# Backward part of a decode step on one NeuronCore: V blocks that TensorE transposes, taken as 32-bit words

## The chip, the cores and the metric

The program runs on one NeuronCore of a Trainium2 chip. A core has TensorE (PE, matrix products; its weight loads are listed as PEld), VectorE (DVE), ScalarE (ACT), GpSimd (POOL) and SyncE (SP), which here issues nearly all of the transfers between the device memory (HBM) and the on-chip memory (SBUF). PE writes its products to a small accumulator memory (PSUM). The metric is the device time of one execution, in microseconds.

## The reference

One decode step of a transformer block: layer norm, attention of one query per head over a cache of 4096 keys and values, a gated feed-forward part, and all gradients of it. Four sequences, 32 heads, head size 128, all in bf16:

```python
scores = jnp.einsum("bhqd,bhkd->bhqk", q, k_cache) * (Dh ** -0.5)
p = _softmax(scores, axis=-1)
o = jnp.einsum("bhqk,bhkd->bhqd", p, v_cache)
return ... @ wo
...
h = x + _A_ref(_layernorm(x), k_cache, v_cache, wq, wo)
h2 = h + _B_ref(_layernorm(h), w1, w3, w2)
```

What is returned is `h2` and the gradients for the input, both caches and all weights. The gradient of the V cache is, for each of the 128 pairs of sequence and head, the outer product of P (4096 numbers) and dO (128 numbers). The gradient of the K cache is the outer product of dS and q, with dS = P * (dP - c) * scale, where dP is the product of the head's V (4096 x 128) with dO, and c is one number for a head. A head's K, V and each of its two cache gradients hold 1 MB. So 128 MB of K are read once, 128 MB of V twice (once in the forward part, once for dP), and 256 MB of gradients are written.

## The kernel before

SBUF holds an arena of 23 slots of about 1 MB (`Slot`); a pair of neighbouring slots (`Slot2`) takes 2 MB. The order of the work on each engine is the order of the program text; every engine and SP's transfer queue go through their own list in that order and wait where data or space is missing. Which slot a tile gets is settled when the program is made, by the age of the free slots.

The forward part, up to about 655 us, streams K and V. A middle part (to about 703 us) computes the feed-forward part and the gradient dO for the first eight heads of each sequence. The backward part follows, and the change lies in it.

Heads 0 to 31 (`SP = 32`) are handled one at a time, the other 96 as 48 pairs. For a head, `load_V2` loads V with SBUF partition p holding rows 32p to 32p+31, so that a partition has 32 blocks of 128 numbers. dP needs the 128 numbers of a row across the partitions. `V_T` (L800, L801) does this: in each of four groups, PE transposes eight 128x128 blocks of bf16 into one PSUM tile (`pt_tps`, two buffers), and ACT copies the tile back over the blocks in the same slot. `front` then multiplies (L1230): eight matmuls of 512 columns, four of them side by side in strips of 32 output rows, with a window of `zd` as the stationary operand. That window is zero but for the columns into which POOL copied dO (`dO_window`, L1195), two heads ahead; so each head adds its rows to one accumulator `dP_ps`, which four heads share.

After four heads `rows_out` (L1205, ACT) copies the accumulator to SBUF, `rows_T` (L1212, PE) transposes it back in four 128x128 blocks of fp32, and `group_dS` (L1247, L1250, DVE) makes dS of four heads. `grad_V` and `grad_K` (L806, DVE) form the outer products in a free slot, and SP writes them out (L817, L1257). For them POOL doubles each number of P (`P_pairs`, L1200), and PE with ACT replicate rows of dO and q (L1179, L1182).

For a pair of heads `load_pair` (L1282) brings 2 MB: the first 64 partitions hold one head, the others the second, 64 blocks on each partition. The first 32 blocks go through PE as above (`front_pair`, L1322, L1323, then row products L1337 with windows `zt`, filled by `dO_pair`, L1292). The other 32 blocks are transposed by DVE in 32x32 pieces of 32-bit words (`rest_pair`, L1343), and PE multiplies them from there (L1349), reading every second number of bf16, with stationaries `zd` that POOL fills with masked dO (`dO_quad`, L1312). `group_dS_pair` (DVE L1359, L1367, L1372 and POOL L1369) makes dS of two pairs, `grad_pair` (L1424) the outer products of 2 MB (written at L1434). Small pieces of other gradients run between these steps on PE and ACT (`side`, L978, L984, L1000).

The main loop calls, for head s: the load of head s + 5, `front(s + 5)`, `more_V` (gradients of V up to eight heads ahead), `grad_K(s)`. It starts with `dO_window(0)`, `dO_window(1)`, three `P_pairs` and five fronts. Head 0's V is transposed already in the middle part.

Of the kernel before, what the change touches and what calls it, by code (L numbers as in the profile page):

```python
# [9 lines left out]
FP32 = mybir.dt.float32  # L10
BF16 = mybir.dt.bfloat16
# [10 lines left out]
SP = 32  # L22
# [5 lines left out]
def kernel(  # L28
# [761 lines left out]
    V2s, VTs = {}, {}  # L790


    def V_T(s, ps, part=range(SJ // GW)):
        if s not in VTs:
            VTs[s] = V2s.pop(s)
        v = VTs[s].heads()
        for g in part:
            pt = ps.tile([P, GW, P], BF16, tag="tps", name="pt_tps")
            for i in range(GW):
                nc.tensor.transpose(pt[:, i, :], v[:, g * GW + i, :], ident_b[:])  # L800
            nc.scalar.copy(out=v[:, g * GW:(g + 1) * GW, :], in_=pt[:])  # L801

    P2s, first_gv = {}, []

# [160 lines left out]
    with ExitStack() as c2:  # L965
# [218 lines left out]

        rows = {}
        dS2s = {}
        zd = [bw3.tile([P, 136], BF16, name=f"zd{i}", tag=f"zd{i}", bufs=1) for i in range(B)]
        dOp = bw3.tile([P, 4, (NH - SP) // 2], BF16, name="dOp", tag="dOp", bufs=1)
        quads = bw3.tile([P, 4], BF16, name="quads", tag="quads", bufs=1)
        for i in range(B):  # L1190
            nc.gpsimd.memset(zd[i][:], 0.0)

        def dO_window(s):
            if s < SP:
                nc.gpsimd.tensor_copy(out=zd[s % B][:, 32:132:67], in_=dOT_bf[:, s:s + 1].to_broadcast([P, 2]))  # L1195

        def P_pairs(s):
            if s < SP and s not in P2s:
# [15 lines left out]
        def front(s):  # L1214
            hl = s % B
            if s not in VTs:
                for g in range(SJ // GW):
                    V_T(s, psT, range(g, g + 1))
                    if hl == 0 and g == 0:
                        rows_out()  # L1220
                    if hl == 0 and g == 2:
                        rows_T()
            VT = VTs[s].heads()
            if hl == 0:
                rows["acc"] = psD.tile([P, 512], FP32, tag="dP", name="dP_ps")
            dO_window(s + 2)
            for u in range(2):
                for c in range(4):
                    j0 = 8 * c + 4 * u
                    nc.tensor.matmul(rows["acc"][32 * c:32 * (c + 1), :], lhsT=zq_window(zd[hl], 2 * hl + u),  # L1230
                                     rhs=VT[:, j0:j0 + 4, :], start=(hl == 0 and u == 0),
                                     stop=(hl == B - 1 and u == 1), tile_position=(0, 32 * c))
            if hl == B - 1:
                rows["ps"] = rows.pop("acc")
            sl = VTs.pop(s)
            if nv["next"] < SP and len(V2s) + len(VTs) + len(vring) < NV2:
                vring.append(sl.i)
            else:
                gave(sl.i, stored=False)

        def group_dS(g):
            i0 = g * B
            T = rows.pop("T").rearrange("p jj (c m) -> p c m jj", c=4)
            t = rows.pop("t")[:, 0:B * SJ].rearrange("p (b j) -> p b j", b=B)
            t5 = t.rearrange("p b (c u jj) -> p b c u jj", c=4, u=2)
            for hl in range(B):
                nc.vector.tensor_scalar(out=t5[:, hl], in0=T[:, :, 2 * hl:2 * hl + 2, :], scalar1=c_rep[:, i0 + hl:i0 + hl + 1],  # L1247
                                        scalar2=scale, op0=ALU.subtract, op1=ALU.mult)
            dS2s[g] = bw3.tile([P, B, SJ, 2], BF16, tag="dS2", name="dS2", bufs=1)
            nc.vector.tensor_tensor(out=dS2s[g][:], in0=t[:, :, :, None].to_broadcast([P, B, SJ, 2]),  # L1250
                                    in1=P_all[:, i0:i0 + B, :, None].to_broadcast([P, B, SJ, 2]), op=ALU.mult)
# [37 lines left out]
        def dO_pair(t):  # L1289
            if t < NT:  # L1290
                s, s2 = two(t)
                nc.gpsimd.tensor_copy(out=zt[t % B][:, 32:34], in_=dOT_bf[:, s:s2 + 1:B])  # L1292

        def dO_quads():
            with nc.allow_low_precision("sums of ones and zeros"):
# [6 lines left out]
            for a in range(2):  # L1302
                r_ = slice(64 * a, 64 * (a + 1))
                nc.scalar.copy(out=dOp[r_].rearrange("p k (i l) -> p k i l", l=B),
                               in_=ps[r_].rearrange("p k (i a l) -> p a k i l", a=2, l=B)[:, a])
            for z in zd:
                nc.gpsimd.memset(z[:], 0.0)

        def dO_quad(t):
            if t < NT:  # L1310
                for k in range(2):
                    nc.gpsimd.tensor_tensor(out=zd[2 * (t % 2) + k][:, 3:131].rearrange("p (q c) -> p q c", c=32)[:, :, 16:24:4],  # L1312
                                            in0=dOp[:, None, 2 * k:2 * k + 2, t].to_broadcast([P, 4, 2]),
                                            in1=quads[:, :, None].to_broadcast([P, 4, 2]), op=ALU.mult)

        def front_pair(t, mid):
            pl = t % 2
            v = pV[t].t[:, 0:2 * SJ * Dh].rearrange("p (j d) -> p j d", d=Dh)
            for g in range(SJ // GW):
                pt = psT.tile([P, GW, P], BF16, tag="tps", name="pt_tps")  # L1320
                for i in range(GW):
                    nc.tensor.transpose(pt[:, i, :], v[:, g * GW + i, :], ident_b[:])  # L1322
                nc.scalar.copy(out=v[:, g * GW:(g + 1) * GW, :], in_=pt[:])  # L1323
                if pl == 0 and g == 0:
                    rows_out()
                if pl == 0 and g == 2:
                    rows_T()
                if g == 3:
                    mid()
            if pl == 0:  # L1330
                rows["acc"] = psD.tile([P, 512], FP32, tag="dP", name="dP_ps")
            dO_pair(t + 2)
            for u in range(2):
                m = 4 * pl + 2 * u
                for c in range(4):
                    j0 = 8 * c + 4 * u
                    nc.tensor.matmul(rows["acc"][32 * c:32 * (c + 1), :], lhsT=zt[t % B][:, 32 - m:64 - m], rhs=v[:, j0:j0 + 4, :],  # L1337
                                     start=(pl == 0 and u == 0), stop=False, tile_position=(0, 32 * c))

        def rest_pair(t):  # L1340
            pl = t % 2
# [3 lines left out]
            for g in range(2):  # L1345
                for r in range(2):
                    for k in range(2):
                        z0 = 3 + 4 * k - 2 * pl - g
                        nc.tensor.matmul(rows["acc"][:], lhsT=zd[2 * pl + r][:, z0:z0 + P], rhs=v5[:, 16 * g:16 * (g + 1), r, :, k],  # L1349
                                         start=False, stop=(pl == 1 and g == 1 and r == 1 and k == 1))  # L1350
            if pl == 1:
                rows["ps"] = rows.pop("acc")
# [1 line left out]
            dO_quad(t + 2)  # L1354

        def group_dS_pair(g):
            T = rows.pop("T").rearrange("p jj (c z l u a) -> p z l a c u jj", c=4, z=4, l=2, u=2, a=2)
            sb = rows.pop("t")
            nc.vector.transpose(out=sb[:], in_=sb[:])  # L1359
            R = sb.rearrange("p (j w) -> p w j", w=32)  # L1360
            t = dSt[0].rearrange("p (l j) -> p l j", l=2)
            t5 = t[:, :, 0:SJ].rearrange("p l (c u jj) -> p l c u jj", c=4, u=2)
            t4 = t[:, :, SJ:2 * SJ].rearrange("p l (g j) -> p l g j", g=2)
            for l in range(2):
                for a, s in enumerate(two(2 * g + l)):
                    r_ = slice(64 * a, 64 * (a + 1))
                    nc.vector.tensor_scalar(out=t5[r_, l], in0=T[r_, 0, l, a], scalar1=c_rep[r_, s:s + 1],  # L1367
                                            scalar2=scale, op0=ALU.subtract, op1=ALU.mult)
                    nc.gpsimd.tensor_scalar(out=t4[r_, l], in0=R[r_, 16 + 2 * l:18 + 2 * l], scalar1=c_rep[r_, s:s + 1],  # L1369
                                            scalar2=scale, op0=ALU.subtract, op1=ALU.mult)  # L1370
            pdS[g] = bw3.tile([P, 2, 2 * SJ, 2], BF16, tag="dS2", name="dS2", bufs=1)
            nc.vector.tensor_tensor(out=pdS[g][:], in0=t[:, :, :, None].to_broadcast([P, 2, 2 * SJ, 2]),  # L1372
                                    in1=P_two(2 * g)[:, :, :, None].to_broadcast([P, 2, 2 * SJ, 2]), op=ALU.mult)

        Pp, zt, P2b, dSt = {}, [], [], []

        def P_two(t, n=2):
# [2 lines left out]
        def P_rows(q):  # L1380
            if q >= NT // B or q in Pp:
                return
            if not Pp:
                Pp["s"] = Slot("Pp")
                x = Pp["s"].t[:, NT * 2 * SJ:]
                zt.extend(x[:, 66 * i:66 * (i + 1)] for i in range(B))
                nc.gpsimd.memset(x[:, 0:66 * B], 0.0)
                P2b.extend(x[:, n:n + 4 * SJ].rearrange("p (j t) -> p j t", t=2) for n in (66 * B, 66 * B + 4 * SJ))
                n = 66 * B + 8 * SJ
                dSt.append(x[:, n:n + 8 * SJ].bitcast(FP32))  # L1390
            Pp[q] = True
            ps = psrep.tile([P, B, 2, SJ], FP32, tag="rep", name="Pp_ps")
            s = SP + q * 2 * B
# [79 lines left out]
        def side(s):  # L1473
# [4 lines left out]
            elif s >= O0:  # L1478
                step("q")

        for s in range(2):
            dO_window(s)
        for s in range(3, 6):
# [11 lines left out]
        for s in range(SP):  # L1495
# [10 lines left out]
                front(s + L)  # L1506
            elif (s + L - SP) % 2 == 0:
                if s + L == SP:
                    dO_pair(0)
                    dO_pair(1)  # L1510
                    dO_quads()
# [64 lines left out]
```

## Time and profile before

| what | value |
|---|---|
| median of three runs | 1697.74 us (1696.97 to 1698.1) |
| profiled execution, its own time | 1696.35 us |
| its span, first to last instruction | 1694.5 us |
| PE, DVE, ACT, POOL busy | 1204.6, 1347.7, 780.1, 538.5 us |
| moved | 707.25 MB (422.59 MB read, 282.34 MB written), mean 417 GB/s |
| mean granted clock of PE | 0.832 |
| transposes of V in the backward part | L800: 1024, 84.3 us; L1322: 1536, 160.6 us |
| copies behind them | L801: 128, 122.1 us; L1323: 192, 186.2 us |

In a group's line the columns are: source line, engine, operation, destination and sources with their shapes, count; then busy time and mean duration in ns; then how long the engine stood idle just before such instructions, and what ended that. In a line of the order in time, the columns are start, length, engine, line, operation, and in brackets the idle time before it. A number after an x counts instructions that were merged into the line. Matmuls overlap, so a merged line is shorter than the sum of its instructions. DMA stands for the transfer engines; a share near 1 means that all sixteen were busy.

### The profile page before, as it was taken

To read this page: it belongs to the slowest core of one execution; us is meant where nothing else is said; L and a number is where in the kernel's file an instruction comes from. 1 tells how busy PE (TensorE), PEld (TensorE's weight loads), DVE (VectorE), ACT (ScalarE), POOL (GpSimd) and SP (SyncE) were. 2 spreads that over 40 slices of the span, in tenths; PEclk is the share of its full clock that TensorE was granted. 3 is DMA by queue.
4 is the path that set the end of the run, shared out by engine and by line. 5 is a ranking of instruction groups with operands and counts; after the bars stand their busy time and mean duration, and the time that the engine had idled before them with its cause. 6 is when DMAs were issued, how large, how long until landed. Compare 5 with 4: busy or idle time off the path is not lost.

```text
span 1694.5 us, 34930 instructions
## 1 busy us (share of the span) xinstructions
PE 1204.6 (71%) x14708; PEld 859.8 (51%) x14708; DVE 1347.7 (80%) x1271; ACT 780.1 (46%) x1300; POOL 538.5 (32%) x779
## 2 busy tenths in 40 slices
PE   5989888888888888878886746656565575575550
PEld 4777766677676766656664533433232333233230
DVE  5999899999999997667767779698677687587585
ACT  3455444454455544677764333434342443344330
POOL 1211223222222222223331436454353345154110
PEclk9999999999999999799879668776667666656675
DMA  9999999999999999999999999999999999999997
GB/s 402 424 424 424 424 424 425 423 424 423 414 424 413 424 412 397 393 412 425 425 426 428 429 420 429 430 429 431 430 427 431 429 413 430 430 410 429 409 382 299
DMA packets 80988, 707.25 MB, mean 417 GB/s; under 512 B 8748, under 2 KB 12984, under 8 KB 15296
## 3 DMA queue, kind: packets, MB, share of 16 engines
q1 hardware_dynamic: 80416, 704.94, 99.1%
q8 instruction: 115, 1.88, 0.4%
q14 instruction: 41, 0.34, 0.0%
q0 software_dynamic: 416, 0.10, 0.0%
HBM read 422.59 MB, written 282.34 MB: 416 GB/s over the span
## 4 chain that ended last, share of the span: by engine, by line
DMA 35%; DVE 8%; ACT 4%; PE 4%; issue 3%; POOL 1%; DVEq 0%; SPq 0%; POOLq 0%; ACTq 0%
DMA out_dram<-arena 34%; DVE arena L1424 6%; ACT arena L801 4%; DMA arena<-in_A_v_cache_dram 2%; PE pt_tps L800 1%; DVE arena L1343 1%; PE dq_ps L1000 1%; PE dP_ps L1230 1%; DVE arena L806 1%; POOL arena L1369 1%; PE pt_wo L610 0%; DVEq L1571 0%; PE rep_ps L1179 0%; PE pt_tps L1322 0%; PE dP_ps L1349 0%
## 5 line engine op out<-in xcount | busy, mean ns | idle before, releaser
L472 PE MATMUL M_ps<-arena 128*128 128x130 bf16 x4096 | 284.7, 222 | 48.9 <-DMA arena<-in_A_v_cache_dram 48.4
L457 DVE TENSOR_TENSOR arena<-arena 128x4096 bf16<-128x4096 bf16 x128 | 292.4, 2284 | 23.5 <-POOL arena L453 23.5
L1323 ACT COPY arena<-pt_tps 128x1024 bf16<-128x1024 bf16 x192 | 186.2, 1024 | 245.5 <-PE pt_tps L1322 245.3
L1424 DVE TENSOR_TENSOR arena<-dS,arena 128x8192 bf16<-128x8192 bf16 x48 | 211.5, 4408 | 100.1 <-DMA out_dram<-arena 100.1
L472 PEld LDWEIGHTS <-arena 128*128 128x128 bf16 x4096 | 250.8, 99 | 70.9 <-DMA arena<-in_A_v_cache_dram 65.1
L1322 PE MATMUL pt_tps<-ident_b,arena 128*128 128x128 bf16 x1536 | 160.6, 280 | 157.2 <-DMA arena<-in_A_v_cache_dram 135.2
L1424 DVE TENSOR_TENSOR arena<-arena 128x8192 bf16<-128x8192 bf16 x48 | 212.2, 4421 | 57.3 <-DMA out_dram<-arena 57.3
L364 DVE STREAM_TRANSPOSE arena<-arena 128x512 f32<-128x512 f32 (+1 forms) x321 | 250.5, 797 | 0.0
L1312 POOL TENSOR_TENSOR zd<-dOp,quads 128x8 bf16<-128x8 bf16 x96 | 151.1, 1589 | 268.6 <-PE dP_ps L1349 266.5
L1322 PEld LDWEIGHTS <-arena 128*128 128x128 bf16 x1536 | 139.6, 130 | 188.1 <-DMA arena<-in_A_v_cache_dram 151.4
L359 ACT COPY arena<-pt_tps 128x1024 bf16<-128x1024 bf16 x128 | 129.4, 1012 | 194.1 <-PE pt_tps L358 154.9
L1349 PE MATMUL dP_ps<-arena,zd 128*128 128x512 bf16 x384 | 145.7, 545 | 83.4 <-DVE arena L1343 83.3
L453 POOL COPY arena<-P_all 128x64 bf16<-128x64 bf16 x128 | 32.4, 253 | 412.4 <-ACT P_all L447 409.4
L370 POOL TENSOR_TENSOR W<-qrep,wmask 128x128 bf16<-128x128 bf16 x128 | 119.5, 933 | 86.5 <-PE S_ps L390 71.7
L801 ACT COPY arena<-pt_tps 128x1024 bf16<-128x1024 bf16 x128 | 122.1, 1026 | 30.4 <-PE pt_tps L800 28.8
L1349 PEld LDWEIGHTS <-zd 128*128 128x128 bf16 x384 | 45.5, 123 | 164.3 <-issue 149.4
L978 ACT CAST arena<-gps 128x512 bf16<-128x512 f32 x110 | 60.5, 585 | 124.4 <-PE gps L984 124.4
L1343 DVE STREAM_TRANSPOSE arena<-arena 128x2048 f32<-128x2048 f32 x48 | 110.5, 2301 | 0.7 <-DMA arena<-in_A_v_cache_dram 0.7
L800 PE MATMUL pt_tps<-ident_b,arena 128*128 128x128 bf16 x1024 | 84.3, 240 | 24.1 <-ACT arena L801 23.9
L1421 POOL COPY arena<-arena 128x128 bf16<-128x128 bf16 x48 | 70.2, 1462 | 67.4 <-ACT arena L1398 63.0
L800 PEld LDWEIGHTS <-arena 128*128 128x128 bf16 x1024 | 72.9, 110 | 34.7 <-issue 33.2
L806 DVE TENSOR_TENSOR arena<-dS,arena 128x4096 bf16<-128x4096 bf16 x32 | 72.9, 2285 | 16.3 <-DMA out_dram<-arena 16.1
(256 smaller groups left out, 1891.3 us busy)
## 6 DMA issues: line engine op xcount, KB each, us to landing
out_dram<-arena SPq DMA_DIRECT2D x96, 2048.0 KB, 27.7
arena<-in_A_v_cache_dram SPq DMA_DIRECT2D x160, 1024.0 KB, 16.1
arena<-in_A_k_cache_dram SPq DMA_DIRECT2D x128, 1024.0 KB, 15.7
arena<-in_A_v_cache_dram SPq DMA_DIRECT2D x48, 2048.0 KB, 27.0
out_dram<-arena SPq DMA_DIRECT2D x72, 1024.0 KB, 20.1
arena<-in_A_wq_dram SPq DMA_DIRECT2D x8, 1024.0 KB, 14.4
arena<-in_B_w_dram SPq DMA_DIRECT2D x8, 896.0 KB, 14.4
out_dram<-arena SPq DMA_DIRECT2D x6, 896.0 KB, 27.8
```

Of the source, the lines that this page charges most:

```text
L359: nc.scalar.copy(out=KT[:, c * GW:(c + 1) * GW, :], in_=pt[:])
L364: nc.vector.transpose(out=KT[:, c * w_:(c + n) * w_], in_=Kn[:, c * w_:(c + n) * w_])
L457: nc.vector.tensor_tensor(out=PK[:, :, 0:Dh].rearrange("p j (r t) -> p j r t", t=2), in0=Ks[s].heads().rearrange("p j (r t) -> p j r t", t=2),
L472: nc.tensor.matmul(hold["M"][:], lhsT=Vn[:, j, :], rhs=PK[:, j, :], start=(j == 0), stop=(j == SJ - 1))
L800: nc.tensor.transpose(pt[:, i, :], v[:, g * GW + i, :], ident_b[:])
L801: nc.scalar.copy(out=v[:, g * GW:(g + 1) * GW, :], in_=pt[:])
L1312: nc.gpsimd.tensor_tensor(out=zd[2 * (t % 2) + k][:, 3:131].rearrange("p (q c) -> p q c", c=32)[:, :, 16:24:4], in0=dOp[:, None, 2 * k:2 * ...
L1322: nc.tensor.transpose(pt[:, i, :], v[:, g * GW + i, :], ident_b[:])
L1323: nc.scalar.copy(out=v[:, g * GW:(g + 1) * GW, :], in_=pt[:])
L1343: nc.vector.transpose(out=v.bitcast(FP32), in_=v.bitcast(FP32))
L1349: nc.tensor.matmul(rows["acc"][:], lhsT=zd[2 * pl + r][:, z0:z0 + P], rhs=v5[:, 16 * g:16 * (g + 1), r, :, k], start=False, stop=(pl == 1 ...
L1424: nc.vector.tensor_tensor(out=dst.rearrange("p (j r t) -> p j r t", r=Dh // 2, t=2), in0=col2[:, :, None, :].to_broadcast([P, 2 * SJ, Dh / ...
```

## The change

V blocks that PE transposes are taken as 32-bit words: two neighbouring bf16 numbers are moved as one. A group of eight blocks of 128 bf16 is then four blocks of 128 words, each made of two rows of V. So a group needs four transposes of fp32 type (with the fp32 identity) in place of eight of bf16, into the same PSUM tile of the same number of bytes. ACT copies the same 1024 bf16 numbers per partition, now back over four separate runs of 256 numbers: group g takes every fourth block of words, starting with g.

After this a partition holds one pair of numbers of one of two rows, i = 0 in the first 64 partitions and i = 1 in the others. The row products read every second number (`words_of`, k = 0 or 1), still eight matmuls of 512 columns for a head. Their stationaries change: dO is split into its even and odd numbers, on both halves of the partitions. A new helper `dO_words` makes this with four small matmuls and an ACT copy, once for the 32 single heads before the first window, and once for the other 96 before the first pair. `dO_window` and `dO_pair` fill a window with two copies on POOL, one per half of the partitions, where one copy did it before. The single heads' windows have fixed columns instead of being cut at a sliding offset.

`group_dS` and `group_dS_pair` read the transposed rows in another order, with the same number of elements. Some small tiles in the slot `Pp` move. The half of a pair's V that DVE transposes is left as it was.

```diff
+    def words_T(ps, v, g):
+        w = v.bitcast(FP32).rearrange("p (x r) -> p x r", r=Dh)
+        pt = ps.tile([P, GW, P], BF16, tag="tps", name="pt_tps")
+        ptw = pt.rearrange("p a b -> p (a b)").bitcast(FP32).rearrange("p (x q) -> p x q", q=P)
+        for jj in range(4):
+            nc.tensor.transpose(ptw[:, jj, :], w[:, 4 * jj + g, :], ident_f[:])
+        nc.scalar.copy(out=v.rearrange("p (x n) -> p x n", n=2 * Dh)[:, g:16:4], in_=pt.rearrange("p (x i) d -> p x (i d)", i=2))
+
+    def words_of(v, g, k):
+        return v.rearrange("p (x r t) -> p t x r", r=Dh, t=2)[:, k, g:16:4]
...
         for g in part:
-            pt = ps.tile([P, GW, P], BF16, tag="tps", name="pt_tps")
-            for i in range(GW):
-                nc.tensor.transpose(pt[:, i, :], v[:, g * GW + i, :], ident_b[:])
-            nc.scalar.copy(out=v[:, g * GW:(g + 1) * GW, :], in_=pt[:])
+            words_T(ps, VTs[s].t[:, 0:SJ * Dh], g)
...
+        def dO_words(dst, s0, s1):
+            ps = psrep.tile([P, 2, s1 - s0], FP32, tag="rep", name="dOw_ps")
+            for k in range(2):
+                for i in range(2):
+                    nc.tensor.matmul(ps[64 * i:64 * (i + 1), k, :], lhsT=ident_b[:, k:P:2], rhs=dOT_bf[:, s0:s1],
+                                     start=True, stop=True, tile_position=(0, 64 * i))
+            nc.scalar.copy(out=dst, in_=ps[:])
 
         def dO_window(s):
             if s < SP:
-                nc.gpsimd.tensor_copy(out=zd[s % B][:, 32:132:67], in_=dOT_bf[:, s:s + 1].to_broadcast([P, 2]))
+                for i in range(2):
+                    r_ = slice(64 * i, 64 * (i + 1))
+                    nc.gpsimd.tensor_copy(out=zd[s % B][r_, :, 2 * (s % B) + i], in_=dOw[r_, :, s])
...
-            for u in range(2):
+            for k in range(2):
                 for c in range(4):
-                    j0 = 8 * c + 4 * u
-                    nc.tensor.matmul(rows["acc"][32 * c:32 * (c + 1), :], lhsT=zq_window(zd[hl], 2 * hl + u),
-                                     rhs=VT[:, j0:j0 + 4, :], start=(hl == 0 and u == 0),
-                                     stop=(hl == B - 1 and u == 1), tile_position=(0, 32 * c))
+                    nc.tensor.matmul(rows["acc"][32 * c:32 * (c + 1), :], lhsT=zd[hl][:, k, :], rhs=words_of(v, c, k),
+                                     start=(hl == 0 and k == 0), stop=(hl == B - 1 and k == 1), tile_position=(0, 32 * c))
...
         def dO_pair(t):
             if t < NT:
                 s, s2 = two(t)
-                nc.gpsimd.tensor_copy(out=zt[t % B][:, 32:34], in_=dOT_bf[:, s:s2 + 1:B])
+                for i in range(2):
+                    r_ = slice(64 * i, 64 * (i + 1))
+                    nc.gpsimd.tensor_copy(out=zt[t % B][r_, :, ZP + 2 * i:ZP + 2 * i + 2], in_=zt[B][r_, :, s - SP:s2 - SP + 1:B])
...
             for g in range(SJ // GW):
-                pt = psT.tile([P, GW, P], BF16, tag="tps", name="pt_tps")
-                for i in range(GW):
-                    nc.tensor.transpose(pt[:, i, :], v[:, g * GW + i, :], ident_b[:])
-                nc.scalar.copy(out=v[:, g * GW:(g + 1) * GW, :], in_=pt[:])
+                words_T(psT, v, g)
...
+        dO_words(dOw, 0, SP)
         for s in range(2):
             dO_window(s)
...
                 if s + L == SP:
+                    dO_words(zt[B], SP, NH)
                     dO_pair(0)
                     dO_pair(1)
```

## The prediction

> **What bounds the kernel now.** I read the page's transfer rows first, then a table by stage, then the instruction groups of the lines the change touches, and last the instructions around the start of the backward part in order of time.
>
> The page's slices and queues:
>
> ```profile
> DMA  9999999999999999999999999999999999999997
> GB/s 402 424 424 424 424 424 425 423 424 423 414 424 413 424 412 397 393 412 425 425 426 428 429 420 429 430 429 431 430 427 431 429 413 430 430 410 429 409 382 299
> ...
> q1 hardware_dynamic: 80416, 704.94, 99.1%
> q8 instruction: 115, 1.88, 0.4%
> ```
>
> The transfer engines are busy nearly everywhere; 707.25 MB at 425 GB/s is 1664 us of a 1694.5 us span. The table by stage (columns: window, its length, then PE, PE's weight loads, DVE, ACT, POOL busy with counts, the granted clock, DMA share, GB/s):
>
> ```profile
> 690.00:725.00 35.00, 27.33 (x402) 20.70 (x400) 24.83 (x29) 23.05 (x29) 13.30 (x22) 0.85 0.95 372
> 725.00:950.00 225.00, 173.08 (x1794) 125.38 (x1793) 154.75 (x106) 141.69 (x164) 61.98 (x71) 0.88 1.01 426
> 950.00:1350.00 400.00, 238.59 (x1803) 140.63 (x1801) 305.72 (x171) 157.91 (x204) 186.68 (x163) 0.71 1.01 429
> 1350.00:1600.00 250.00, 151.53 (x932) 81.57 (x932) 183.30 (x95) 102.05 (x147) 97.77 (x98) 0.64 1.00 423
> 1600.00:1694.50 94.50, 31.37 (x190) 15.08 (x189) 70.16 (x35) 15.62 (x21) 11.23 (x21) 0.61 0.82 342
> ```
>
> From 725 to 1600 us, where nearly all the changed work lies, the share is full (1.00 to 1.01): an engine that gets faster or slower there moves nothing while the transfers stay queued. Only two stretches are open: the start, 690 to 725 us, which moved 372 GB/s, and the last 94 us. In 5 us slices the start fell to 362, 377, 421, 318, 413, 400 and 311 GB/s from 690 us on, without full queues in most of them. Against 425 the six short slices lack 63+48+107+12+25+114 = 369 GB/s times 5 us, 1.85 MB, or 4.3 us of transfer. In the last stretch DVE is busy for 70 us of the 76 us up to its last instruction (outer products, L1424, 4.4 us each), so TensorE has slack there: the last row transposes L1212 end at 1651.9 us, and the DVE instruction that follows them in the program starts at 1659.8 us.
>
> The groups (mean ns of one after the busy time):
>
> ```profile
> L1322 PE MATMUL pt_tps<-ident_b,arena 128*128 128x128 bf16 x1536 | 160.6, 280 | 157.2 <-DMA arena<-in_A_v_cache_dram 135.2 <-ACT arena L1323 22.0
> ...
> L800 PE MATMUL pt_tps<-ident_b,arena 128*128 128x128 bf16 x1024 | 84.3, 240 | 24.1 <-ACT arena L801 23.9
> ...
> L1212 PE MATMUL dPT_ps<-ident_f,dPr 128*128 128x128 f32 x128 | 27.3, 352 | 0.7 <-ACT dPr L1205 0.7
> ```
>
> The reader is to see that the trace already holds the new operation: L1212 transposes a 128x128 block of 32-bit values, four to a PSUM tile.
>
> **The change part by part.** Transposes: 32 single heads and 48 pair halves have four groups each, 320 groups; each goes from 8 transposes of 16-bit blocks to 4 of 32-bit blocks. A group of L1322 keeps PE busy 160.6/192 = 0.836 us, of L800 84.3/128 = 0.659 us; a group of four at L1212 27.3/32 = 0.853 us. L1212 ran 8 groups in the single-head stage and 24 in the pairs, so its like is (8 x 0.659 + 24 x 0.836)/32 = 0.792 us: +0.06 us a group, +20 us of PE busy time in all. I take that. It costs nothing at the end because ACT's copies set the pace: L801 and L1323 take 1.02 us and follow each other every 0.94 us. In the shortest (warm) form both kinds fit below that, 0.61 us for eight and 0.66 us for four. In the pairs PE sat idle 135 us for V to arrive. Were that cover gone, the 0.05 us of a warm group would show once per head, 0.25 us over the five first heads.
>
> The same loads seen through a rule: TensorE: Matmul & The Clock Gate, section "Weight-path perf modes — Fast Weight Load (FWL) and DoubleRow", in the Trainium skill says that the fast load of weights is off for 32-bit data, and that it was measured at about 2 times; by it a word block loads twice as long, half as often, and the sum is 0. The rows say 188 ns against 110 and 130 ns, 1.4 to 1.7 times, which agrees roughly in kind and would be a small gain on the loads alone.
>
> Copies out of PSUM: same 1024 elements, now written in four runs of 256 with gaps. L254's copies of the weight tiles, written in two runs, took 1015 ns against 1024 and 1026: nothing. They write into the tile that later transposes still read. The same pattern stands at L601, whose two-run units kept PE going without a wait for L254 (PE idle 0.2 us or less in 112), so I take no new wait.
>
> Row products: L1230 and L1337 keep their count, 8 per head, width 512, but read every second 16-bit element. L390 has both readings with 32 output rows: every second element (W) median 282 ns, runs (zq) median 273 ns for 256 columns. Bounds 0 and +9 ns (+18 for 512 columns); 8 x 18 ns = 0.14 us a head at most, hidden as above. The gradient tensor_scalars L1247 and L1367 read the same 32 elements from PSUM in another order: 242 and 248 ns for both existing patterns, taken at nothing. They end before L1250 and L1372, and DVE waits for transfers 157 us in all at L1424.
>
> Windows on POOL: dO_window and dO_pair become two copies on half the partitions. That is 32 + 48 more POOL copies. L1195 has min 185, median 192, max 2264 ns; L1292 174, 438, 4377. So each costs 0.19 to 2.3 us in the single heads (the long ones last as long as an L806 outer product, 2285 ns mean) and 0.17 to 4.4 us in the pairs. Behind them on POOL wait the pair copies L1200 and L1421, which the outer products L806 and L1424 read, and later the window's own matmuls. Windows are written two heads ahead and the pair copies one or two ahead, so past 725 us it is hidden by full queues and by POOL's idle time (POOL waits 266 us for PE at L1312 alone).
>
> The start is not covered. First the order there:
>
> ```profile
> 702.32 0.66 POOL L1191 MEMSET zd<- 128x136 bf16 x4
> 702.94 0.31 POOL L1195 COPY zd<-dOT_bf 128x2 bf16<-128x2 bf16 x2
> 703.18 0.14 PEld L1230 LDWEIGHTS <-zd 128*32 128x32 bf16 x8 [2.65 <-POOL zd L1195]
> ...
> 704.44 2.29 DVE L806 TENSOR_TENSOR arena<-arena 128x4096 bf16<-128x4096 bf16 x1 [2.03 <-PE dP_ps L1230]
> ```
>
> Memset, window, first row products, then the next gradient product in the space that they free: each waits for the one before, and transfers run dry a moment later (318 GB/s from 705 us). One extra copy of 0.19 us stands in this line: +0.2 us. The new dO_words (four small matmuls, like four of L1300's 16 in 0.35 us, then an ACT copy of about 0.3 us like L1304) fits in PE's idle 2.5 us and ACT's 3.1 us there; bounds 0 and +0.7 us, its whole length. I take 0, nearest to those gaps. Five further extra copies fall in the five first fronts, beside DVE outer products without gaps. Bounds: 0 if each runs while DVE waits anyway, 5 x 2.26 = 11.3 us if each holds the next product back a full length. L806 waited for POOL only 1.9 us in two instances here, and a copy that runs as DVE stands costs 0.19: I take half of 5 x 0.19, +0.5 us.
>
> A rule against the change: SBUF — State Buffer, section "Terms", in the Trainium skill says VectorE and GpSimd share a port pair which the holder keeps for a whole instruction while the other is blocked. The maxima 2264 and 4377 ns agree; by the rule alone the start would pay up to the 11.3 us, by the medians 1 us.
>
> The second dO_words stands before the first pair (about 908 us): four matmuls, a copy, then dO_quads reuses the same PSUM tile: about 1 us later on PE, with share 1.01 and V loaded ahead, nothing. No transfer is added, removed or moved on SP's queue. The instruction queue shrinks: 2 x 1280 records of PE less, about 100 more of PE, ACT and POOL, 7% of 34930; 7% of its 0.4% (6.8 us) is -0.5 us.
>
> Sum: +0.2 + 0.5 - 0.5 = +0.2 us. On the profiled execution (1696.35 us, span 1694.5) that is 1696.55; the median of the runs shown is 1.39 us above that execution, so 1697.9 us.
>
> **The rivals.** *POOL holds the outer products at the start* (slower): three of five extra copies each cost a whole outer product, 3 x 2.26 = 6.8 us, 1704.7 us. For it: copies of 2.23 to 2.26 us already stand one after another between 711 and 721 us. Against: two heads of lead, and DVE waits that let POOL catch up in 0.2 us steps. It decides from two such copies (4.5 us).
>
> *The copies in place stop PE* (slower): if each transpose group waited for the copy before it, a group would take 0.66 + 1.02 us and about 0.2 us between, 1.9 against 0.94, 3.8 us a head; over five heads 19 us, half of it shown by the short queues, about 1707.5 us. The L601 rows speak against.
>
> *PE's front gets ahead at the start* (faster): PE's loads at L800 waited 33.2 us in 60 instances for their own issue; with half the instructions up to 0.55 us a head goes, and slots come free sooner. The most it can return is the lack of 4.3 us: 1693.6 us. Against: ACT still paces.
>
> *The 32-bit form saves no PE time* is part of the forecast, so its failing gives nothing: even 100 us less PE between 725 and 1600 us would lie below full transfers.
>
> **How the numbers follow.** No change seen 0.56; POOL at the start 0.15; copies in place 0.08; front ahead 0.15; something unseen 0.06 (0.04 slower, 0.02 faster). A measurement of this kernel tells about 0.2% (3.4 us) from no change. Faster 0.17, same 0.56, slower 0.27. The likeliest alone spans 1696.5 to 1700. The range goes down to 1693.5, the whole lack at the start returned, and up to 1704.0, short of three blocked copies; outside lie the copies in place, some 0.06 of POOL's case and most of the unseen, 0.18.
>
> **What would show it.** Right: transposes at 1280, PE busy 0 to 30 us more, L801 and L1323 still at 1.02 us and 0.94 us apart, DMA share 1.01 from 725 us, first row products at 703.3 to 703.6 us, the window copies twice as many. Wrong: PE waiting for ACT more than once a group; L806 waiting for POOL for more than 3.4 us before 725 us; a lower share in the middle; or transfers that themselves run at another rate, which no step here has.

## The result and the profile after

The changed kernel takes 1841.26 us (median of 5 runs, 1839.95 to 1842.91) against 1696.97 us before (median of 5 runs, the three of the table above among them): 1.0853 times as long, 95% interval 1.0837 to 1.0869. It was forecast at 1697.9 us with a range to 1704.0.

The page's slices of the profiled execution after (span 1839.4 us, a slice is 46 us):

```profile
PE   5889888888888896666666667665776576666650
PEclk8999999999999995555555557787556756666565
DMA  9999999999999997777677679999999999999998
GB/s 403 424 424 423 424 424 424 423 423 420 422 413 424 412 397 303 250 253 260 244 250 293 255 278 363 425 426 429 427 429 428 431 429 429 432 430 430 430 430 344
```

Ten slices, from about 690 to 1150 us, lie at 244 to 363 GB/s; the slices around them are as they were. In the first nine of the ten PE's granted clock is 0.5. The stages (window, length, busy time of PE, PE's loads, DVE, ACT and POOL with counts, clock, DMA share, GB/s):

```profile
690.00:725.00 35.00, 22.61 (x242) 16.14 (x239) 20.75 (x22) 14.57 (x18) 16.51 (x25) 0.55 0.81 335
725.00:950.00 225.00, 146.06 (x770) 100.04 (x769) 89.39 (x69) 94.36 (x102) 59.41 (x58) 0.50 0.71 249
950.00:1350.00 400.00, 270.48 (x1532) 163.85 (x1532) 266.80 (x157) 163.79 (x194) 139.99 (x165) 0.63 0.88 360
1350.00:1600.00 250.00, 167.20 (x742) 75.23 (x742) 189.28 (x100) 105.65 (x142) 106.75 (x121) 0.62 1.01 429
```

DVE's work from 725 to 950 us fell from 154.75 to 89.39 us and the rate from 426 to 249 GB/s: the heads come later. The transposes' group of the page shows why:

```profile
L798 PE MATMUL pt_tps<-ident_f,arena 128*128 128x128 f32 x1280 | 320.8, 398 | 284.7 <-ACT arena L799 243.0
```

PE waited 243.0 us for ACT's copies, in 239 instances: three of the four groups in each of 80 fronts (32 heads, 48 pairs) are 240. Before, the two lines together waited 45.9 us for ACT. The order in time shows one head (start, length, engine, line; in brackets the idle time before it):

```profile
805.30 1.01 ACT L799 COPY arena<-pt_tps 128x1024 bf16<-128x1024 bf16 x1 [1.55 <-PE pt_tps L798]
...
806.37 1.12 PE L798 MATMUL pt_tps<-ident_f,arena 128*128 128x128 f32 x4 [1.10 <-ACT arena L799]
807.52 1.01 ACT L799 COPY arena<-pt_tps 128x1024 bf16<-128x1024 bf16 x1 [1.21 <-PE pt_tps L798]
...
808.59 1.11 PE L798 MATMUL pt_tps<-ident_f,arena 128*128 128x128 f32 x4 [1.10 <-ACT arena L799]
...
813.02 1.05 PE L1248 MATMUL dP_ps<-arena,zd 128*32 128x512 bf16 x8 [1.10 <-ACT arena L799]
```

Group and copy take turns: a pitch of 2.2 us. Before, a group waited only for the copy two back, ACT copied without a break, and the pitch was 3.76/4 = 0.94 us:

```profile
711.12 3.76 ACT L801 COPY arena<-pt_tps 128x1024 bf16<-128x1024 bf16 x4 [1.28 <-PE pt_tps L800]
712.18 0.61 PE L800 MATMUL pt_tps<-ident_b,arena 128*128 128x128 bf16 x8 [0.70 <-ACT arena L801]
713.10 0.61 PE L800 MATMUL pt_tps<-ident_b,arena 128*128 128x128 bf16 x8 [0.31 <-ACT arena L801]
```

After, the row products wait for the last copy too. First and last row products of the single heads start at 705.0 and 1076.4 us, 371.4/31 = 12.0 us a head; before, at 703.2 and 907.1 us, 203.9/31 = 6.6 us. Three transfers of a head, 3.15 MB, need 7.4 us at 425 GB/s. So the heads' chain has become the bound of its stage: 32 x (12.0 - 7.4) = 147 us, against 144 us lost.

SP's own queue shows how that empties the transfers (line, what it waited for: us in total, times, longest). The first line is from 725 to 1075 us after, the second, the same load, from 725 to 950 us before:

```profile
SPq L840 <- PE dP_ps L1248: 217.5, 23, 11.8
SPq L833 <- PE dP_ps L1230: 12.1, 4, 4.6
```

So SP stood 217.5 us at a load of V whose slot the row products had not given free; the gradients to be written stand behind it in the same queue.

Where the wait is from stands in the programs' instruction lists, in which every instruction has its waits before the program runs. PE's list for one head after (head 1; x3 stands for three more of the same; of the row products only the first is shown):

```
L798 Matmult pt_tps 128x128 [waits DMA, DVE]    L798 x3
L798 Matmult pt_tps 128x128 [waits Activation]  L798 x3
L798 Matmult pt_tps 128x128 [waits Activation]  L798 x3
L798 Matmult pt_tps 128x128 [waits Activation]  L798 x3
L1248 Ldweights zd [waits Pool]
L1248 Matmult dP_ps 32x512 [waits Activation]
```

Two PSUM tiles in turn ask for a wait at the third and fourth group, for the copy two back. The wait at the second group is new, and so is what the others wait for: the copy just before. That copy and the group behind it share no block and no PSUM tile.

### The profile page after: what moved, and what is told of

Same layout as the page of the kernel before. It is cut to its first block, busy times and chain, and to the rows that moved or that the text cites. A ratio compares the mean times of both kernels' runs of the same rounds, so it can differ in the third digit from the quotient of the medians.

```text
span 1839.4 us, 32572 instructions
## 1 busy us (share of the span) xinstructions
PE 1317.6 (72%) x13436; PEld 888.4 (48%) x13436; DVE 1346.4 (73%) x1271; ACT 799.9 (43%) x1302; POOL 556.3 (30%) x859
## 5 line engine op out<-in xcount | busy, mean ns | idle before, releaser
L798 PE MATMUL pt_tps<-ident_f,arena 128*128 128x128 f32 x1280 | 320.8, 398 | 284.7 <-ACT arena L799 243.0
L799 ACT COPY arena<-pt_tps 128x1024 bf16<-128x1024 bf16 x320 | 323.9, 1012 | 415.6 <-PE pt_tps L798 408.0
L798 PEld LDWEIGHTS pt_tps<-ident_f,arena 128*128 128x128 f32 x1280 | 210.2, 201 | 389.6 <-ACT arena L799 327.4
L472 PEld LDWEIGHTS <-arena 128*128 128x128 bf16 x4096 | 252.3, 99 | 61.7 <-DMA arena<-in_A_v_cache_dram 55.2
L1331 POOL TENSOR_TENSOR zd<-dOp,quads 128x8 bf16<-128x8 bf16 x96 | 123.5, 1303 | 296.2 <-PE dP_ps L1363 296.0
L359 ACT COPY arena<-pt_tps 128x1024 bf16<-128x1024 bf16 x128 | 129.4, 1012 | 187.0 <-PE pt_tps L358 154.5
L1311 POOL COPY arena<-arena 64x4 bf16<-64x4 bf16 x96 | 97.3, 1014 | 51.4 <-ACT arena L1208 47.7
L1214 POOL COPY zd<-dOp 64x2 bf16<-64x2 bf16 x64 | 62.3, 974 | 137.9 <-PE dP_ps L1248 135.8
L1264 DVE TENSOR_SCALAR dPr<-dPT_ps,c_rep 128x32 f32<-128x32 f32 x32 | 5.8, 244 | 120.6 <-PE dPT_ps L1231 120.6
L813 DVE TENSOR_TENSOR arena<-P,arena 128x4096 bf16<-128x4096 bf16 x29 | 66.0, 2287 | 21.0 <-DMA out_dram<-arena 10.5
```

The costliest lines, as they stand in the source:

```text
L359: nc.scalar.copy(out=KT[:, c * GW:(c + 1) * GW, :], in_=pt[:])
L472: nc.tensor.matmul(hold["M"][:], lhsT=Vn[:, j, :], rhs=PK[:, j, :], start=(j == 0), stop=(j == SJ - 1))
L798: nc.tensor.transpose(ptw[:, jj, :], w[:, 4 * jj + g, :], ident_f[:])
L799: nc.scalar.copy(out=v.rearrange("p (x n) -> p x n", n=2 * Dh)[:, g:16:4], in_=pt.rearrange("p (x i) d -> p x (i d)", i=2))
L813: nc.vector.tensor_tensor(out=dst.rearrange("p j (r t) -> p j r t", t=2), in0=col2[:, :, None, :].to_broadcast([P, SJ, Dh // 2, 2]), in1=r ...
L1331: nc.gpsimd.tensor_tensor(out=zq_[2 * (t % 2) + k][:, 3:131].rearrange("p (q c) -> p q c", c=32)[:, :, 16:24:4], in0=dOp[:, None, 2 * k:2 ...
```

## The experiments

All times are medians, ratios are to the kernel before on the same chip (medians of 1695.74 to 1695.87 us there). W is the theory that the copies' wait is the cause; P that the window copies on POOL are; T that the 32-bit transposes themselves are.

**Groups in one run.**

```diff
-            nc.tensor.transpose(ptw[:, jj, :], w[:, 4 * jj + g, :], ident_f[:])
-        nc.scalar.copy(out=v.rearrange("p (x n) -> p x n", n=2 * Dh)[:, g:16:4], in_=...)
+            nc.tensor.transpose(ptw[:, jj, :], w[:, 4 * g + jj, :], ident_f[:])
+        nc.scalar.copy(out=v[:, g * GW * Dh:(g + 1) * GW * Dh], in_=...)
...
-    [:, k, g:16:4]
+    [:, k, 4 * g:4 * g + 4]
```

> The changed kernel with one thing altered: a group takes four neighbouring blocks of words, so that ACT copies it back in one run of 1024 numbers; the row products and dS read in the matching order. Word transposes, window copies on POOL, dO_words and the reading of every second number all stay. Theory W (each transpose group waits for the copy before it, because the copies in runs that lie between the next group's blocks are taken to touch them): the waits of PE for ACT fall from 239 to about 160 short ones, a group's pitch from 2.24 to about 0.95 us, and the time to 1697.9 us, give or take 4. Rival P (the window copies on POOL hold the heads up): stays above 1830. Rival T (32-bit transposes are slow by themselves, 398 ns, and keep PE at half clock): stays above 1800.

1689.74 us, ratio 0.9964 (0.9951 to 0.9978): slightly faster than before, its five runs (1688.85 to 1690.52) below all of before's. The transposes' waits for ACT are back from 243.0 to 46.0 us, in 112 instances, and the single heads' stage has its clock and its rate again. The order in time shows the pairs of groups running on, and the waits of two buffers in turn, as before:

```profile
L798 PE MATMUL pt_tps<-ident_f,arena 128*128 128x128 f32 x1280 | 257.2, 356 | 170.3 <-DMA arena<-in_A_v_cache_dram 124.2 <-ACT arena L799 46.0
...
725.00:950.00 225.00, 176.76 (x1327) 118.08 (x1326) 156.19 (x108) 142.61 (x166) 84.92 (x102) 0.87 1.01 427
...
743.85 1.07 PE L798 MATMUL pt_tps<-ident_f,arena 128*128 128x128 f32 x8
745.58 0.66 PE L798 MATMUL pt_tps<-ident_f,arena 128*128 128x128 f32 x4 [0.67 <-ACT arena L799]
746.08 0.65 PE L1231 MATMUL dPT_ps<-ident_f,dPr 128*128 128x128 f32 x4
746.99 0.66 PE L798 MATMUL pt_tps<-ident_f,arena 128*128 128x128 f32 x4 [0.26 <-ACT arena L799]
```

P and T fall: all their work is in this kernel. Of the 8 us below the expected 1697.9, some 2 lie in the kernel before, which has 1695.74 us on this chip; the other 6 are taken up further down.

**The kernel before, written in eight runs.** Group g takes every fourth block, with 16-bit transposes.

```diff
-                nc.tensor.transpose(pt[:, i, :], v[:, g * GW + i, :], ident_b[:])
-            nc.scalar.copy(out=v[:, g * GW:(g + 1) * GW, :], in_=pt[:])
+                nc.tensor.transpose(pt[:, i, :], v[:, 4 * i + g, :], ident_b[:])
+            nc.scalar.copy(out=v[:, g:SJ:4, :], in_=pt[:])
```

> The kernel before with 16-bit transposes, but group g takes every fourth block of 128 numbers, so its copy is written in eight runs between the blocks of the other groups; row products and dS follow that order. If runs that lie apart are enough for the wait (W in its plain form): PE waits for ACT before three of four groups, the heads take about 12 us each, 1830 us or more. If the wait needs a copy that counts 16-bit numbers against a read that counts 32-bit words: no such wait, 1697 us, give or take 3. P and T expect 1697 too. Should eight runs cost ACT time, its copies go above 1.02 us.

1697.06 us, ratio 1.0004 (0.9995 to 1.0013). The transposes' waits for ACT are 25.7 us in the heads and 19.6 in the pairs, where they were 23.9 and 22.0. Runs that lie apart do no harm by themselves, and they cost ACT nothing: its copies take 1.02 us.

**Copies of words, still apart.** One line of the changed kernel:

```diff
-        nc.scalar.copy(out=v.rearrange("p (x n) -> p x n", n=2 * Dh)[:, g:16:4], in_=pt.rearrange(...))
+        nc.scalar.copy(out=w[:, g:16:4], in_=ptw)
```

> The changed kernel with one line altered: ACT's copy keeps its four runs apart but is written as 512 words of 32 bits in place of 1024 numbers of 16. Reader and writer then count in the same unit. W in the form left by the last runs (the wait arises where runs that lie apart are written in 16-bit numbers and the neighbours are read as 32-bit words): no wait before the second group, ACT's copy about 0.59 us like the 128x512 fp32 copies, heads under 5 us, 1690 us give or take 4. If runs apart with words are enough: waits stay, the pitch falls only by the shorter copy to about 1.8 us, a head to about 10.5 us, and the time is 1770 to 1800 us.

1690.43 us, ratio 0.9969 (0.9960 to 0.9979). The wait is gone though the runs lie as in the changed kernel: the transposes wait for ACT's copies 19.4 us in all, and the instruction list of the head above has its first eight transposes in one piece. Together with the two runs before it this settles the condition: a copy in runs apart, written as 16-bit numbers, beside reads of the same slot as 32-bit words. Runs apart alone (the kernel before in eight runs, and this one) make no wait, nor do the two units alone (groups in one run). Why the tool that places the waits does so, perhaps because it judges the two views by their outer bounds, is not shown; the runs show only the condition.

**Copies of words, in one run.**

```diff
-        nc.scalar.copy(out=v[:, g * GW * Dh:(g + 1) * GW * Dh], in_=pt.rearrange("p a d -> p (a d)"))
+        nc.scalar.copy(out=w[:, 4 * g:4 * g + 4], in_=ptw)
```

> The groups in one run, with copies of 512 words. If transfers bound the time once the waits are gone, half of ACT's copy time (320 copies by 0.43 us, 138 us) is worth nothing but at the start, where a head's chain gets about 1.5 us shorter and at most the 4.3 us lack of transfers is returned: 1686 to 1690 us. If the copies on ACT still set the pace in the single heads: 1680 us or less.

1689.75 us, ratio 0.9963 (0.9950 to 0.9977), the same as with 16-bit copies. A copy fell from 1023 ns there to 589 ns:

```profile
L799 ACT COPY arena<-pt_tps 128x512 f32<-128x512 f32 x320 | 182.1, 589 | 352.9 <-PE pt_tps L798 352.4
```

127 us less work on ACT (182.1 against 309.0) is worth nothing that the time shows; in the single heads' stage the transfers have a share of 1.01 in both kernels.

**Apart in the single heads alone.** A flag picks the form for each stage; the row products read every fourth block in both.

```diff
-            words_T(ps, VTs[s].t[:, 0:SJ * Dh], g)
+            words_T(ps, VTs[s].t[:, 0:SJ * Dh], g, True)
...
-                words_T(psT, v, g)
+                words_T(psT, v, g, False)
```

> The changed kernel with copies in four runs for the 32 single heads alone; in the pairs a copy goes back in one run. W with the stage deciding: a head needs 7.4 us of transfers (3 MB) and its chain on PE and ACT about 12.3 us with the waits, so nearly the whole loss is here: 1825 to 1842 us. If the loss came evenly from all 320 groups, 40% of it: about 1755 us.

1834.13 us, ratio 1.0817 (1.0802 to 1.0831). 40% of the groups carry nearly the whole loss (138 us).

**Apart in the pairs alone**, the two flags exchanged.

> The counterpart: copies in four runs for the 48 pairs alone, in one run for the single heads. A pair needs 14.8 us of transfers and its chain with waits is 4 times 2.24 for the groups, 1.1 and 3.6 us for row products, about 1 us for others, 14.7 us: at the edge. W with the stage deciding: 1698 to 1712 us. If the loss came evenly from all groups, 60% of it: about 1784 us.

1707.56 us, ratio 1.0059 (1.0034 to 1.0084), with runs from 1688.53 to 1712.73. The loss showed in an unexpected place:

```profile
725.00:950.00 225.00, 179.26 (x1171) 137.01 (x1169) 133.68 (x96) 130.77 (x150) 81.62 (x88) 0.64 0.99 388
```

That is the single heads' stage, whose copies were in one run here (the profiled execution took 1711.26 us). But its row products still read every fourth block. Two further runs take this apart.

**Copies in one run everywhere, row products over all four groups**, so that all eight wait for the last copy: the one edit of the first experiment without its second half.

> Copies in one run in heads and pairs, but a strip's row products still read every fourth block of words, so all eight of a head wait for the last copy. With pairs apart the single heads had lost rate too (388 GB/s from 725 to 950 us, clock 0.64), though their copies were in one run. If these late row products drop the clock and push a head past its 7.4 us of transfers: clock under 0.75 in that stage and 1695 to 1710 us, with a wide spread. If the loss there came from the waits in the pairs: the clock stays near 0.87 and the time is 1690 us give or take 2.

1698.47 us, ratio 1.0018 (1.0005 to 1.0031), runs from 1693.49 to 1705.75; in the profiled one (1693.87 us) clock 0.71 and 410 GB/s in that stage. The row products waited 36.7 us for ACT in 31 instances, against 16.6 in 32 with groups in one run. So one late wait of about 1.2 us per head goes with a lower clock and costs some 9 us. Why the runs of this kernel and of the last spread so widely is not shown, as one run of each was profiled; of the last, the fastest had the highest mean clock (0.801) and the six slowest 0.777 to 0.781.

**Apart in the pairs, all in one run in the heads.**

```diff
+    words_T(psT, v, g, True)                 # pairs: every fourth block
+    rhs=words_of(v, c, k, True)
```

> Copies and row products in one run for the single heads, in runs apart for the 48 pairs alone; 144 of the 240 waits stay. Theory (a wait costs only where a stage's chain is longer than its transfers, 14.7 us against 14.8 for a pair): 1690 to 1700 us, full rate from 725 to 950 us. If waits cost alike everywhere: about 1777 us.

1688.44 us, ratio 0.9957 (0.9944 to 0.9969). PE's transposes wait for ACT 169.7 us in 199 instances, and it costs nothing:

```profile
725.00:950.00 225.00, 175.34 (x1318) 115.27 (x1317) 156.33 (x110) 143.50 (x166) 85.57 (x100) 0.87 1.01 427
950.00:1350.00 400.00, 260.69 (x1396) 136.62 (x1398) 308.85 (x172) 164.33 (x204) 184.48 (x190) 0.67 1.01 430
```

Against groups in one run, the late row products alone cost some 9 us, the waits in the pairs alone nothing, and both together (the run with the pairs apart) some 16 us by the ratios. What the other 7 us come from stays open.

**Work for PE while it waits: transposes.** They write into the tile that the group overwrites.

```diff
+        for jj in range(4):
+            nc.tensor.transpose(ptw[:, jj, :], ident_f[:], ident_f[:])
```

> The changed kernel with its waits, plus four transposes of the fp32 identity before each group, which PE can run while it waits for ACT's copy. They write to the tile that the group then overwrites. Theory: part of the loss is the clock, 0.50 from 700 to 1075 us, because PE stands for half of each 2.24 us. If filling the gaps brings the clock up: groups of 0.66 us, a pitch of about 1.85 us, a head near 10 us, 1765 to 1790 us. If transposes don't count as work that raises the clock, or the stand-still is not what lowers it: clock 0.50 still, 1841 us or up to 20 more for the filler of each first group.

**The same with plain matmuls.**

```diff
+        for jj in range(2):
+            nc.tensor.matmul(ptw..., lhsT=ident_b[:], rhs=P_all[:, 0:16, :], start=True, stop=True)
```

> The same with two plain bf16 matmuls of 512 columns before each group in place of the four transposes: 0.43 us of PE at full clock, 0.85 at half. If the clock follows how much PE works, as with the transposes: 1765 to 1790 us. If matmuls raise the clock and transposes do not, this kernel is faster than the one with transposes by about 50 us or more. If the clock has nothing to do with the gaps: 1841 to 1860 us in both.

1790.22 us (ratio 1.0563, 1.0543 to 1.0582) and 1782.03 us (1.0507, 1.0493 to 1.0522): 51 and 59 us faster than the changed kernel, by adding work. The stage from 725 to 950 us, with transposes (profiled at 1796.91 us, the slowest of four runs) and with matmuls:

```profile
725.00:950.00 225.00, 169.27 (x1245) 134.19 (x1244) 92.38 (x72) 106.99 (x115) 57.85 (x64) 0.81 0.80 282
```

```profile
725.00:950.00 225.00, 163.46 (x1064) 103.88 (x1082) 95.06 (x75) 108.55 (x117) 59.01 (x61) 0.82 0.82 293
```

The clock rises from 0.50 to 0.81 and 0.82. Groups at full clock take 0.66 us in place of 1.11, and a wait behind each stays:

```profile
807.92 0.66 PE L800 MATMUL pt_tps<-ident_f,arena 128*128 128x128 f32 x4 [0.72 <-ACT arena L801]
```

A head takes 10.6 and 10.3 us (first to last row products, 706.7 to 1034.4 and 703.6 to 1023.7 us). So over a third of the loss went through the clock, which the waits themselves had lowered. Transposes raised it as matmuls did, with 8 us between the two; the second idea of the expectation, 50 us between them, falls.

**The kernel before with two window copies on POOL.**

```diff
-                nc.gpsimd.tensor_copy(out=zd[s % B][:, 32:132:67], in_=dOT_bf[:, s:s + 1]...)
+                for r_ in (slice(0, 64), slice(64, 128)):
+                    nc.gpsimd.tensor_copy(out=zd[s % B][r_, 32:132:67], in_=dOT_bf[r_, s:s + 1]...)
```

The same in dO_pair.

> The kernel before with one part of the change alone: each window is filled by two POOL copies on half the partitions. The prediction's term was +0.7 us, at most +11.3. Theory: 0 to +1 us against before, within what can be told. If POOL copies were what gains 6 us with groups in one run (an accident of order): 1690 us. If they hold outer products at the start: 1702 us or more.

1696.78 us, ratio 1.0004 (0.9995 to 1.0012): no cost that can be told.

**Groups in one run, with four tiny matmuls a group.**

```diff
+        for jj in range(4):
+            nc.tensor.matmul(ptw[:, jj, 0:1], lhsT=ident_b[:], rhs=ident_b[:, 0:1], start=True, stop=True)
```

> The groups in one run, with four matmuls of one column before each group, which bring the PE instructions back to about the count before (1280 loads and 1280 matmuls more). They write to the tile that the group then overwrites. If the 6 us gained against before come from fewer instructions (fewer of them to bring in, 115 packets against 106): 1694 to 1697 us. If they come from something else: 1690 us give or take 2.

1696.26 us, ratio 1.0005 (0.9996 to 1.0014). The gain of the first experiment is gone; the instruction queue is back from 106 packets to 115. This agrees with the idea that fewer PE instructions gave the 6 us. Of the kernels without a loss in the single heads, the four with 106 packets (groups in one run, both with word copies, pairs apart with heads in one run) lie at 1688 to 1690 us, and those with 115 (before, its two variants, and this one) at 1696 to 1697. The cause is not shown by that alone: the tiny matmuls also load weights (87.3/320 = 0.27 us a group), and the clock from 690 to 725 us fell from 0.85 to 0.71. 0.14 MB of instructions would take 0.3 us at 425 GB/s, so their bytes alone don't explain it. The tables place the gain behind the single heads: 369 against 372 GB/s from 690 to 725 us and 427 against 426 to 950 us, but 430 against 429 to 1350 us and 427 against 423 to 1600 us. How fewer instructions would do that stays open.

## Why the prediction was wrong

The step that failed: "They write into the tile that later transposes still read. The same pattern stands at L601, whose two-run units kept PE going without a wait for L254 (PE idle 0.2 us or less in 112), so I take no new wait." L601 and L254 both count 16-bit numbers. The changed kernel writes 16-bit numbers and reads 32-bit words. The row was near in shape and differed in the one thing that decided. What the runs showed in its place: PE waited 243.0 us for ACT in 239 instances, nearly one before each group but the first of a front, and a head went from 6.6 to 12.0 us, above its 7.4 us of transfers. Groups in one run, the kernel before in eight runs, and copies of words show the condition of the wait. Of the prediction's signs of being wrong, the lower share in the middle was seen: 0.71 and 0.88 where it was 1.01.

The right rival had 0.08 and the wrong price, 1707.5 us. Two terms of its sum were too small.

- Its pitch was taken as 1.9 us with a warm group of 0.66 us. Measured: 2.2 us, as the clock fell to 0.50 and a group took 1.11 us. The table before had shown a clock of 0.88 in this stage, a quantity that I took as given though the change acts on it.
- It was charged for five heads only, "half of it shown by the short queues". The cover for the others was that past 725 us "the transfers stay queued". That cover holds only while the chain is shorter than its transfers: 12.0 us a head against 7.4 empties it, for all 32 heads. With the rival's own 3.8 us a head on the 6.6 us of before, the comparison of the stage's chain with its transfers would have given (10.4 - 7.4) x 32 = 96 us; the two runs with filler, most of whose groups are at full clock, lost 94 and 86 us. With the measured 12.0 us it gives 147 us.

What the waits do to the clock was left out there. In the Trainium skill, TensorE: Matmul & The Clock Gate, section "Why this matters for your kernels", advises against gaps of PE above some 3 us. In this stage PE's longest wait was 1.2 us and the clock stayed at 0.50 for 370 us, so here gaps well under that were enough. The same page, section "Part 4: PE-mode transpose", says that transposes do not bring the full clock; here transposes alone, put into the gaps, raised 0.50 to 0.81, so it isn't so in this case.

Point by point for the rest:

- Transposes: +20 us of PE busy time forecast. With groups in one run they took 257.2 us (0.80 us a group) against 84.3 + 160.6 = 244.9, +12 us, and PE was busy for 1226.9 us in all against 1204.6, +22. Somewhat oversized, and hidden, as forecast.
- Reading every second number, the order of dS, dO_words, two window copies: forecast +0.7 us at the start with the copies on POOL; no cost told by the run of the copies alone (0.9995 to 1.0012 of before), and none left in the kernel with groups in one run. The rival with POOL at the start, 6.8 us, is out.
- "An engine that gets faster or slower there moves nothing while the transfers stay queued": it held for 127 us less of ACT and for the waits in the pairs alone; it failed in the single heads, where they did not stay queued.
- Instructions: -0.5 us forecast. Without the wait the change gains 6.0 us (0.9964), and restoring the count of instructions takes it back. If the count is the cause, which the runs do not settle, the term was twelve times too small.
- PE getting ahead at the start (1693.6 us) did not happen as told: with groups in one run the start still moved 369 GB/s, against 372.

Without the wait, then, the sum was off by 8 us, 2 of them in the level of the kernel before, and with it by 143 us.

## What to carry to other kernels

Where a tile is rewritten in place, do not carry over a row that shows "no wait" unless writer and reader use the same units of data and the same spacing as there; else price the wait by what it does to each stage's chain, and set that chain against the stage's transfers. Give each group one run of memory, or copy in the unit that is read: both cost nothing here and turned 1841 us into 1690. When a chain gets waits, price PE's work at half clock too: here a group went from 0.66 to 1.11 us.

## What the runs showed of the hardware

- PE at half clock through waits of 1.1 us: with a group of 1.11 us and a wait of 1.10 us in turn, the granted clock was 0.50 for 370 us. Four transposes or two matmuls of no use in each gap gave 0.81 and 0.82. Which length or share of idle time decides is not shown.
- Four transposes of 128x128 words take 0.66 us at a granted clock of 1.0 and 1.11 us at 0.5, eight of 16-bit blocks 0.61 and 1.01 us.
- ACT's copy out of PSUM takes 1023 ns as 1024 16-bit numbers and 589 ns as 512 words of the same bytes.
- The two kernels whose single heads have one late wait each make wide runs, 1693.49 to 1705.75 and 1688.53 to 1712.73 us, where groups in one run stay within 1.7 us.
